# The second layer's operands moved by 32 bytes within SBUF, with the order of work left as it is

## The chip, the cores and the metric

One NeuronCore of a Trainium2 chip runs the whole program. The metric is the device time of one execution in microseconds; the kernel before takes 1753.78 us, the median of three runs (1752.92 to 1754.33).

## The reference

Attention whose keys and values are averaged over groups of eight positions, and then two dense layers on its output, all in float32:

```python
# attention: batch 8, heads 8, sequence 576, head size 64
k_p = k.reshape(B, H, S // 8, 8, D).mean(axis=3)
v_p = v.reshape(B, H, S // 8, 8, D).mean(axis=3)
attn = softmax(q @ k_p.T / sqrt(D))
x = (attn @ v_p)            # 4608 tokens x 512
# first layer
h = np.maximum(x @ w1_in, 0.0)      # 512 -> 2048
x = h * h @ w1_out                  # 2048 -> 512
# second layer
h = x @ w2_in
out = np.maximum(0.01 * h, h) @ w2_out
```

## The kernel before

Every float32 operand of a large product is split in two parts, a rounded one ("high") and the remainder ("low"), both stored as four-byte `float32r`. A product is then three passes of TensorE: high by high, low by high, high by low.

**First layer and attention** (to about 990 us). Tokens go in nine blocks of 512. `first` (line 861) makes one chunk of 128 hidden rows by twelve matmuls of 512 columns (line 866), with the weights `wi` as the loaded operand and `xh`, `xl` as the moving one. `second` (line 894) takes the squared chunk `gh`, `gl` as the moving operand and the weights `wo` as the loaded one, again twelve matmuls of 512 columns (line 905). Attention of the next block (transposes of 128 columns in lines 449, 551, 650 and 656 and scores of 144 columns in line 587, all in plain float32; values in lines 701 to 704) stands between them, piece by piece.

**Second layer** (class `Second`, line 1124; from about 994 us to the end). The hidden dimension is taken in two halves, the tokens in six spans of 768, and each half of the weights in four pairs; that makes 48 groups. A group has seven products (`product`, line 1273: a scheme that gets a 2 by 2 block product out of seven smaller ones). Each is six matmuls of 384 columns (line 1280) with `wi` loaded and the sums of token blocks `fh`, `fl` moving: 48 x 7 x 6 = 2016 matmuls. Between the products of a group stand the six pieces of the group before (`piece`, line 1341): each is six matmuls of 512 columns (line 1347) with `sh`, `sl`, the hidden values after the leaky step, loaded and the output weights `wo` moving: 48 x 6 x 6 = 1728 matmuls. ScalarE and VectorE take the products out of PSUM (lines 1293, 1297, 1304), apply the leaky step (line 1321) and split the result (lines 1325, 1328). The order is written out by hand (`manual_schedule`); no planner moves anything.

**Places in SBUF.** Pools on the left grow from the low addresses up, pools on the right from the top down. The top of the right side lies 32 bytes past a multiple of 64. Line 82 puts a tile of 32 bytes (`pad`) there first, so that all the tiles below it start at a multiple of 64. Every operand that TensorE reads, in both layers, then starts at 0 mod 64. The weights' slots `wi0` to `wi7` and `wo0` to `wo3` are used by the first layer and then again by the second (`make_in`, line 1201, and `fetch_out`, line 1232); `sh` and `sl` lie in a pool of their own (`open_work`, line 1141), in the room that `wo4` to `wo7` had.

Of the kernel before, what the change touches and what calls it, by code (L numbers as in the profile page):

```python
# [9 lines left out]
F32 = mybir.dt.float32  # L10
F32R = mybir.dt.float32r
# [5 lines left out]
P = 128  # L17
# [26 lines left out]
def attention_relu2_leaky_kernel(  # L44
# [12 lines left out]
    nc = tc.nc  # L57
# [21 lines left out]
    ).split()  # L79

    common = ctx.enter_context(tc.tile_pool(name="sb", bufs=1, side="left"))
    pad = ctx.enter_context(tc.tile_pool(name="pad", bufs=1, side="right"))
    nc.gpsimd.memset(pad.tile([P, 8], F32, tag="pad", name="pad"), 0.0)
    weights = ctx.enter_context(tc.tile_pool(name="wt", bufs=1, side="right"))
    spare = tc.alloc_tile_pool(name="sp", bufs=1, side="right")
    attn = tc.alloc_tile_pool(name="at", bufs=1, side="left")
    opened = [spare, attn]
    psum = ctx.enter_context(tc.tile_pool(name="ps", bufs=1, space=bass.MemoryType.PSUM))
    dram = ctx.enter_context(tc.tile_pool(name="dr", bufs=1, space=bass.MemoryType.DRAM))

    BUFS = {"raw": 3, "val": 3, "qt": 2, "r": 3, "gh": 2, "gl": 2, "s": 2, "kt": 2, "kp": 2}
    BUFS.update({"m": 4, "l": 4, "st": 3, "val": 2})

    POOLS = {tag: weights for i in range(FC // 2) for tag in (f"wi{i}", f"wo{i}")}
    POOLS.update({f"wo{i}": spare for i in range(FC // 4, FC // 2)})
    POOLS.update({tag: common for tag in "cst raw r gh gl st xh xl".split()})

    def sb(shape, dt, tag):
        pool = POOLS.get(tag, attn)
        return pool.tile(shape, dt, tag=tag, name=tag, bufs=BUFS.get(tag, 1))  # L100

    def bank():
        return psum.tile([P, 512], F32, tag="ps", name="ps", bufs=4)

    def acc_bank(m):
        return psum.tile([P, 512], F32, tag=f"acc{m}", name=f"acc{m}")

    def f32(ap):
        return ap.bitcast(F32)
# [7 lines left out]
    mid = dram.tile([2, FC, P, T], F32, tag="mid", name="mid")  # L117

    cst = sb([P, C_N], F32, "cst")
    ident = cst[:, C_ID : C_ID + P]  # L120

# [6 lines left out]
    def home_tile(shape):  # L128
        return sb(shape, F32, f"wo{late.pop()}")
# [12 lines left out]
    def load_to(key, fn, tag):  # L142
        live[tag] = live.get(tag, 0) + 1
        t = sb([P, 512], F32, tag)
        fn(t)
        raws[key] = t, tag
# [5 lines left out]
    def load(n=99):  # L152
        while n and todo and not held:
            key, fn, tag = todo[0]
            if live.get(tag, 0) == BUFS[tag]:
                return
# [940 lines left out]
    def run(blk):  # L1097

        last = blk == BLOCKS - 1
        steps, turn = [], []  # L1100
        if not last:
            steps, turn = all_steps[blk + 1], value_steps(blk + 1, (blk + 1) * T)

        def chunk_done(what, c):
            if last:
                layer2.early(what, c)
            else:
                w2.tick()
                if blk == BLOCKS - 2 and (what, c) == ("out", FC - 1):
                    w2.finish()  # L1110

        block(blk, blk * T, steps, turn, chunk_done)
# [11 lines left out]
    class Second:  # L1124
# [16 lines left out]
        def open_work(self):  # L1141
# [12 lines left out]
            POOLS.update({"u3": pool, "h11": pool})  # L1154
            BUFS.update({"u3": 2, "h11": 2})
            self.acc = [acc_bank(m) for m in range(KC)] + [bank() for _ in range(2)]
# [44 lines left out]
        def make_in(self, p):  # L1201
            ra, rb = self.words
            sums = sb([P, 4, 2, P], F32, "sums")
            s1, s2, s3, s4 = (sums[:, n] for n in range(4))
            hi = sb([P, 7, 2, P], F32R, f"wi{2 * p}")
            lo = sb([P, 7, 2, P], F32R, f"wi{2 * p + 1}")
            self.weights[p] = hi, lo
            parts = (
                (slice(0, 1), ra[:, :, 0:1].rearrange("p k j f -> p j k f")),
                (slice(1, 3), rb.rearrange("p k j f -> p j k f")),  # L1210
                (slice(3, 7), sums),
            )

            def add(out_, x, y, op):
                return lambda: nc.vector.tensor_tensor(out=out_, in0=x, in1=y, op=op)

            def high(at, x):
                return lambda: nc.scalar.copy(hi[:, at], x)

            sub = ALU.subtract  # L1220
            return (
                [
                    add(s1, ra[:, :, 1], rb[:, :, 1], ALU.add),
                    add(s3, ra[:, :, 0], ra[:, :, 1], sub),
                    add(s2, s1, ra[:, :, 0], sub),
                    add(s4, rb[:, :, 0], s2, sub),
                ]
                + [high(at, x) for at, x in parts]
                + [add(lo[:, at], x, f32(hi[:, at]), sub) for at, x in parts]
            )  # L1230

        def fetch_out(self, half, p):
            t = sb([P, 2, 1024], F32R, f"wo{p}")
            nc.sync.dma_start(out=f32(t), in_=w2_parts[PAIRS * half + p])
            self.outs[p] = t.rearrange("p n (c f) -> p n c f", c=2)

# [164 lines left out]
        def run(self):  # L1401
            opened.pop().release()
            self.open_work()
            for g in range(len(self.groups)):
                self.group(g)
            self.flush()
            for i in range(TT):
                self.piece(len(self.groups) - 1, i)
            while opened:
                opened.pop().release()  # L1410
# [3 lines left out]
    with tc.manual_schedule():  # L1414
        nc.sync.dma_start(out=cst, in_=consts)
        nc.gpsimd.memset(f32(v_rem), 0.0)
        start()
        for s in value_steps(0, 0):
            s()
        pooled.add(1)  # L1420
        held.append(True)
        all_steps = {i: attention_steps(i, i * T, ("raw",)) for i in range(2, BLOCKS)}
        first_products()
        second_products()
        for blk in range(2, BLOCKS):
            run(blk)
        layer2.run()
# [31 lines left out]
```

## Time and profile before

| what | value |
| --- | --- |
| median of three runs | 1753.78 us |
| the profiled execution's own time | 1752.09 us |
| span of its instructions | 1750.2 us |
| TensorE matmuls busy | 1704.1 us, 97% of the span |
| VectorE busy | 1111.6 us, 64% |
| ScalarE busy | 627.7 us, 36% |
| GpSimd busy | 19.0 us, 1% |

The profiled execution took 1752.09 us, of which 1.9 us lie outside the span. A matmul's busy time overlaps the next one's, since they are pipelined; how often TensorE starts a matmul is read from the chain of work, where each stretch of matmuls has its length and its count.

### The profile page before, as it was taken

The numbers are of one execution on the slowest core, as the hardware profiler recorded it, in microseconds if no ns is written. First come the engines' busy times: TensorE is split into PE (matmuls) and PEld (weight loads), VectorE is DVE, ScalarE is ACT, GpSimd is POOL, SyncE is SP. The second block draws the span as 40 slices with busy tenths as digits, with TensorE's granted clock in tenths as the row PEclk, the third lists the DMA queues.
The fourth block names the chain that finished last, engine by engine and source line by source line (L and its number), as shares of the span: only waits on it lengthen the run. The fifth ranks groups of instructions, "written<-read, shape, count | busy, mean of one in ns | idle before, by whom it ended". The sixth has DMA issues, their size and how long they took to land.

```text
span 1750.2 us, 21697 instructions
## 1 busy us (share of the span) xinstructions
PE 1704.1 (97%) x8312; PEld 1462.5 (84%) x8312; DVE 1111.6 (64%) x2020; ACT 627.7 (36%) x1496; POOL 19.0 (1%) x38
## 2 busy tenths in 40 slices
PE   6889999999999999999999999999999999999999
PEld 5768778888888888888888898888888888888987
DVE  7888777666657676565435555565566665666564
ACT  4545333343443433433333322332332332233221
POOL 0012000000000000000000000000000000000000
PEclk9999999999999999999999999999999999999999
DMA  8914552323223232231004202201202411320220
GB/s 235 340 70 144 168 175 93 94 79 99 83 97 104 96 95 78 88 107 61 13 24 159 82 1 73 73 12 61 73 24 97 169 52 57 109 106 9 103 73 37
DMA packets 106296, 162.44 MB, mean 93 GB/s; under 512 B 44112, under 2 KB 44240, under 8 KB 105168
## 3 DMA queue, kind: packets, MB, share of 16 engines
q1 hardware_dynamic: 103632, 152.67, 26.3%
q0 software_dynamic: 2560, 8.39, 1.3%
q8 instruction: 65, 1.06, 0.3%
q14 instruction: 39, 0.32, 0.1%
HBM read 111.75 MB, written 49.28 MB: 92 GB/s over the span
## 4 chain that ended last, share of the span: by engine, by line
PE 90%; DVE 6%; ACT 2%; DMA 1%; issue 1%; SPq 0%; DVEq 0%; ACTq 0%
PE acc L905 20%; PE ps L1280 20%; PE ps L866 17%; PE acc L1347 15%; PE ps L1347 8%; PE acc L866 4%; PE ps L587 2%; PE ps L650 1%; PE ps L551 1%; ACT s L608 1%; PE acc L381 1%; PE ps L702 0%; DMA wi<-in_moe_w_in 0%; PE ps L704 0%; PE ps L701 0%
## 5 line engine op out<-in xcount | busy, mean ns | idle before, releaser
L905 PE MATMUL acc<-gh,wo 128*128 128x512 f32 x1152 | 298.3, 397 | 4.0 <-DVE gh L884 1.9
L866 PE MATMUL ps<-xh,wi 128*128 128x512 f32 x896 | 297.0, 394 | 0.0
L1280 PE MATMUL ps<-fh,wi 128*128 128x384 f32 x1344 | 288.3, 335 | 0.1
L1280 PEld LDWEIGHTS ps<-fh,wi 128*128 128x128 f32 x1344 | 243.1, 188 | 25.4 <-DVE gh L1293 0.4
L905 PEld LDWEIGHTS acc<-gh,wo 128*128 128x128 f32 x1152 | 214.8, 190 | 51.1 <-DVE gh L884 4.0
L1347 PE MATMUL acc<-wo,sh 128*128 128x512 f32 x768 | 208.4, 393 | 0.0
L866 PEld LDWEIGHTS ps<-xh,wi 128*128 128x128 f32 x896 | 168.2, 188 | 34.9 <-issue 0.2
L866 PE MATMUL ps<-xl,wi 128*128 128x512 f32 x448 | 174.5, 389 | 0.0
L884 DVE CAST gh<-r 128x512 fp32r<-128x512 f32 x112 | 47.7, 426 | 199.3 <-ACT r L879 199.0
L1280 PE MATMUL ps<-fl,wi 128*128 128x384 f32 x672 | 170.5, 334 | 0.0
L905 PE MATMUL acc<-gl,wo 128*128 128x512 f32 x576 | 160.8, 393 | 0.0
L1347 PEld LDWEIGHTS acc<-wo,sh 128*128 128x128 f32 x768 | 141.3, 188 | 17.2
L876 ACT ACTIVATE r<-ps 128x512 f32<-128x512 f32 x112 | 67.7, 604 | 212.1 <-PE ps L866 212.1
L905 PEld LDWEIGHTS acc<-gl,wo 128*128 128x128 f32 x576 | 109.3, 190 | 23.5
L1347 PE MATMUL acc<-wo,sl 128*128 128x512 f32 x384 | 121.8, 398 | 0.0
L1280 PEld LDWEIGHTS ps<-fl,wi 128*128 128x128 f32 x672 | 121.3, 188 | 0.0
L608 ACT ACTIVATE s<-ps,m 128x72 f32<-128x72 f32 x240 | 72.3, 331 | 104.7 <-DVE m L599 104.7
L1347 PE MATMUL ps<-wo,sh 128*128 128x512 f32 x384 | 104.2, 393 | 0.0
L1293 DVE TENSOR_TENSOR u<-gh,ps 128x384 f32<-128x384 f32 x48 | 26.6, 554 | 121.8 <-PE ps L1280 121.8
L866 PEld LDWEIGHTS ps<-xl,wi 128*128 128x128 f32 x448 | 84.2, 188 | 16.6
L1347 PEld LDWEIGHTS acc<-wo,sl 128*128 128x128 f32 x384 | 71.9, 187 | 18.9 <-DVE sl L1328 3.0
L885 DVE TENSOR_TENSOR gl<-r,gh 128x512 fp32r<-128x512 f32 x112 | 77.6, 693 | 7.7 <-PE acc L905 0.5
(205 smaller groups left out, 2364.9 us busy)
## 6 DMA issues: line engine op xcount, KB each, us to landing
wi<-in_moe_w_in SPq DMA_DIRECT2D x8, 1024.0 KB
wo<-in_moe_w_out SPq DMA_DIRECT2D x8, 1024.0 KB
val<-in_moe_w_in SPq DMA_DIRECT2D x16, 512.0 KB
val<-in_moe_w_out SPq DMA_DIRECT2D x16, 512.0 KB
w2p<-val SPq DMA_DIRECT2D x16, 512.0 KB
wo<-w2p SPq DMA_DIRECT2D x8, 1024.0 KB
xh<-x SPq DMA_DIRECT2D x10, 768.0 KB
xl<-x SPq DMA_DIRECT2D x10, 768.0 KB
```

The costliest lines, as they stand in the source:

```text
L381: nc.tensor.matmul(ps[:n, c * 2 * D : (c + 1) * 2 * D], lhsT=ident[:n, :n], rhs=raw[:n, r * 2 * D : (r + 1) * 2 * D], start=r == 0, stop=r ...
L551: nc.tensor.transpose(ps[:, cc * P : (cc + 1) * P], raw[:, cc * P : (cc + 1) * P], ident)
L587: nc.tensor.matmul(ps[: r0 + n, c2 * PAIR : (c2 + 1) * PAIR], lhsT=qt[:, cc, : r0 + n], rhs=kts[b][:, keys], start=True, stop=True,)
L608: nc.scalar.activation(out=s[:, g, :], in_=ps[:, h * SP : (h + 1) * SP], func=AF.Exp, bias=m[:, g : g + 1], accum_out=None if i in early e ...
L866: nc.tensor.matmul(ps, lhsT=w[:, kc], rhs=x[kc], start=(kc == 0 and n == 0), stop=(kc == KC - 1 and n == 2),)
L876: nc.scalar.activation(out=r, in_=ps, func=AF.Relu)
L884: nc.vector.tensor_copy(gh, r)
L885: nc.vector.tensor_tensor(out=gl, in0=r, in1=f32(gh), op=ALU.subtract)
L905: nc.tensor.matmul(acc[m], lhsT=w[:, m * P : (m + 1) * P], rhs=x, start=(c == 0 and n == 0), stop=(c == FC - 1 and n == 2),)
L1280: nc.tensor.matmul(at, lhsT=w[:, FORMS[j], kc], rhs=x[j][:, kc], start=m == 0 and j in (0, 1, 4), stop=m == 5, skip_group_check=True,)
L1293: nc.vector.tensor_tensor(out=out_, in0=x, in1=at, op=ALU.add)
L1347: nc.tensor.matmul(self.acc[i], lhsT=x[g % 2][c][t][:, at], rhs=self.outs[p][:, part_, c], start=p == 0 and m == 0, stop=p == PAIRS - 1 an ...
```

## The change

The tile `pad` is left out, so that the right side starts 32 bytes past a multiple of 64. The slots of `wo0` to `wo3` and of `wi3` become 32 bytes longer, and a tile takes its place in such a slot either at its start or 32 bytes further on (`off`, in words of four bytes). A last tile of 32 bytes is added to the pool of `sh` and `sl`, which puts the other tiles of that pool 32 bytes past a multiple of 64; it is set to zero once, on GpSimd, after the first group. The tiles `m` and `l` of attention (maxima and sums, 32 bytes each) get two buffers each in place of four, 128 bytes less in all.

Start of TensorE's operands in the built programs, in bytes past a multiple of 64:

| matmuls | moving, before | moving, after | loaded, before | loaded, after |
| --- | --- | --- | --- | --- |
| line 866 (first layer) | `xh`, `xl`: 0 | 0 | `wi`: 0 | 0 |
| line 905 (first layer) | `gh`, `gl`: 0 | 0 | `wo`: 0 | 0 |
| line 1280 (second layer) | `fh`, `fl`: 0 | 0 | `wi`: 0 | 32 |
| line 1347 (second layer) | `wo`: 0 | 32 | `sh`, `sl`: 0 | 32 |

Taken by 128 bytes, all of them stand at 64 before. After, a quarter of the loads of line 905 (those of `wo2`) start at 0 mod 128; those of line 1280 at 96, the moving operand of line 1347 at 32 for half of the matmuls and at 96 for the other half.

The order of instructions on TensorE, VectorE, ScalarE and the DMA queue of SyncE is the same in both programs, row by row, with the same waits; VectorE and ScalarE each wait once for GpSimd's count of 1 where it was 2. Only on GpSimd does one instruction move. Its start in the program before (`v_rem` is zeroed for attention, `mid` is the first layer's hidden chunks on their way to DRAM):

```order
L1438 MEMSET const-uint8-127 128x1
L1455 UNCONDITIONAL_BRANCH
L83 MEMSET pad 128x8
L1416 MEMSET v_rem 128x512
L1056 DMA mid<-r 128x512 x20
```

The same engine in the changed program, from its start to its end:

```order
L1453 MEMSET const-uint8-127 128x1
L1470 UNCONDITIONAL_BRANCH
L1431 MEMSET v_rem 128x512
L1068 DMA mid<-r 128x512 x20
L1068 DMA mid<-xl 128x512 x4
L1068 DMA mid<-xh 128x512 x4
L1068 DMA mid<-xl 128x512 x4
L1420 MEMSET off 128x8
```

A memset of eight words per partition goes from the start of GpSimd's queue to its end, behind the last of its transfers.

```diff
     common = ctx.enter_context(tc.tile_pool(name="sb", bufs=1, side="left"))
-    pad = ctx.enter_context(tc.tile_pool(name="pad", bufs=1, side="right"))
-    nc.gpsimd.memset(pad.tile([P, 8], F32, tag="pad", name="pad"), 0.0)
     weights = ctx.enter_context(tc.tile_pool(name="wt", bufs=1, side="right"))
...
-    BUFS = {"raw": 3, "val": 3, "qt": 2, "r": 3, "gh": 2, "gl": 2, "s": 2, "kt": 2, "kp": 2}
-    BUFS.update({"m": 4, "l": 4, "st": 3, "val": 2})
+    BUFS = {"raw": 3, "val": 3, "qt": 2, "r": 3, "gh": 2, "gl": 2, "s": 2, "kt": 2, "kp": 2, "m": 2, "l": 2}
+    BUFS.update({"st": 3, "val": 2})
...
-    def sb(shape, dt, tag):
+    OFF = 8
+
+    def sb(shape, dt, tag, off=None):
         pool = POOLS.get(tag, attn)
-        return pool.tile(shape, dt, tag=tag, name=tag, bufs=BUFS.get(tag, 1))
+        if off is None:
+            off = OFF if tag in ("wo1", "wo3") else 0
+        n = int(np.prod(shape[1:]))
+        size = [P, OFF + n] if off or tag == "wi3" else shape
+        t = pool.tile(size, dt, tag=tag, name=tag, bufs=BUFS.get(tag, 1))
+        if size is shape:
+            return t
+        t = t[:, off : off + n]
...
-            hi = sb([P, 7, 2, P], F32R, f"wi{2 * p}")
-            lo = sb([P, 7, 2, P], F32R, f"wi{2 * p + 1}")
+            hi = sb([P, 7, 2, P], F32R, f"wi{2 * p}", OFF)
+            lo = sb([P, 7, 2, P], F32R, f"wi{2 * p + 1}", OFF)
...
-            t = sb([P, 2, 1024], F32R, f"wo{p}")
+            t = sb([P, 2, 1024], F32R, f"wo{p}", OFF * (1 - p % 2))
...
                 self.group(g)
+                if g == 0:
+                    last = opened[-1].tile([P, OFF], F32, tag="off", name="off")
+                    nc.gpsimd.memset(last, 0.0)
```

## Rows read from the trace of the kernel before

**Rows 1.** The page's busy times, share of span and instructions; granted clock in 40 slices.

```profile
PE 1704.1 (97%) x8312; PEld 1462.5 (84%) x8312; DVE 1111.6 (64%) x2020; ACT 627.7 (36%) x1496; POOL 19.0 (1%) x38
...
PEclk9999999999999999999999999999999999999999
```

**Rows 2.** Busy time by stretch, first and second layer: us; engines (instructions); clock, DMA.

```profile
300.00:990.00 690.00, 680.63 (x3235) 565.28 (x3234) 415.06 (x819) 271.36 (x756) 0.00 (x0) 1.00 0.26 83
994.00:1740.00 746.00, 745.91 (x3718) 668.70 (x3717) 450.94 (x795) 218.19 (x408) 0.00 (x0) 1.00 0.19 68
```

**Rows 3.** Who waited for whom from 994 us on: us, times, longest us.

```profile
DVE u L1293 <- PE ps L1280: 170.9, 95, 3.8
ACT sh L1325 <- DVE h L1321: 126.8, 48, 3.0
...
PEld acc L1347 <- DVE sl L1328: 3.0, 11, 0.4
...
PEld ps L1280 <- DVE gh L1293: 0.4, 1, 0.4
```

**Rows 4.** The chain in the second layer: start us, length us, matmuls.

```profile
1401.44 1.39 PE acc L1347 x6
1402.83 1.04 PE ps L1280 x6
1403.87 1.39 PE ps L1347 x6
...
1407.69 2.08 PE ps L1280 x12
1409.78 1.39 PE acc L1347 x6
```

**Rows 5.** The chain at the end of the first layer, with scores and transposes between.

```profile
863.84 0.98 PE ps L587 x8
864.82 2.78 PE ps L866 x12
867.60 2.72 PE acc L905 x12
870.32 2.72 PE ps L866 x12
873.04 2.72 PE acc L905 x12
875.76 0.44 PE ps L551 x4
```

**Rows 6.** The page's groups of the second layer's matmuls and weight loads, with counts.

```profile
L1280 PE MATMUL ps<-fh,wi 128*128 128x384 f32 x1344 | 288.3, 335 | 0.1
L1280 PEld LDWEIGHTS ps<-fh,wi 128*128 128x128 f32 x1344 | 243.1, 188 | 25.4 <-DVE gh L1293 0.4
L1347 PE MATMUL acc<-wo,sh 128*128 128x512 f32 x768 | 208.4, 393 | 0.0
...
L1280 PE MATMUL ps<-fl,wi 128*128 128x384 f32 x672 | 170.5, 334 | 0.0
...
L1347 PE MATMUL acc<-wo,sl 128*128 128x512 f32 x384 | 121.8, 398 | 0.0
...
L1347 PE MATMUL ps<-wo,sh 128*128 128x512 f32 x384 | 104.2, 393 | 0.0
```

**Rows 7.** Single lines, ns min/median/max, first and last start: `pad`, the fetch of `wo`, `sl`.

```profile
L83 POOL MEMSET pad<- x1: 105/105/105, 0.7 to 0.7; 128x8 f32 x1
...
L1234 SPq DMA_DIRECT2D wo<-w2p x8: 319/320/383, 920.5 to 1377.7; - x8
...
L1328 DVE TENSOR_TENSOR sl<-h,sh x48: 549/551/552, 1000.2 to 1733.9; 128x384 fp32r<-128x384 f32 x48
```

More of the change, by code (lines that the diff above doesn't have):

```diff
@@ L96, in attention_relu2_leaky_kernel @@
     POOLS.update({tag: common for tag in "cst raw r gh gl st xh xl".split()})
-    def sb(shape, dt, tag):
+    OFF = 8
+    def sb(shape, dt, tag, off=None):
         pool = POOLS.get(tag, attn)
-        return pool.tile(shape, dt, tag=tag, name=tag, bufs=BUFS.get(tag, 1))
+        if off is None:
[6 more added lines that the diff above has]
+        t = t[:, off : off + n]
+        if len(shape) == 2:
+            return t
+        names = "abcd"[: len(shape) - 1]
+        sizes = {a: k for a, k in zip(names, shape[1:])}
+        return t.rearrange(f"p ({' '.join(names)}) -> p {' '.join(names)}", **sizes)
     def bank():
```

## The prediction

> **What bounds the kernel now.** I read the busy times first, then the two layers apart, then who waits for whom, and last the chain of work, whose stretches give the time from one matmul's start to the next.
>
> TensorE is busy for 97% of the span at its full granted clock [rows 1]. The reader should see where the rest is: in the first layer 680.6 of 690 us, in the second 745.9 of 746 [rows 2]. From 994 us on TensorE never stands still. VectorE and ScalarE are the ones that wait there, for TensorE or for each other, in waits of up to 3.8 us; the two waits that hold up TensorE's weight loads come to 3.4 us in sum, the longest 0.4 us, and none of it shows as idle time of the matmuls [rows 2, 3]. So in the second layer the time is the number of matmuls times their pitch, and no other engine's speed counts until it gets worse by more than those waits.
>
> The pitch comes from the chain. A piece of six matmuls of 512 columns takes 1.39 us, 231.7 ns each; six of 384 columns take 1.04 us, 173.3 each [rows 4]. In the first layer a dozen of 512 columns takes 2.72 us, 226.7 each, once it runs undisturbed; the dozen right behind the scores takes 2.78, 231.7 each, although it reads the same kind of tiles at the same places [rows 5]. From 384 to 512 columns the settled pitch goes from 173.3 to 226.7: 53.4 ns for 128 columns, 0.417 ns a column, one column per clock at 2.4 GHz, the level that the rows grant [rows 2, 4, 5]. At that rate 512 columns are 213.3 ns and 384 are 160. Both leave the same **excess of 13.3 ns**, whatever the columns; and unsettled stretches of 512 leave 18.3.
>
> What the excess hangs on is half visible. Every matmul loads its weights, a load per matmul [rows 1]; the load of 128 columns lasts 188 ns and lies beside the stream of the matmul before [rows 6]. Matmuls in plain float32 have loads too, but stream at half the rate: eight of 144 columns take 0.98 us and four of 128 take 0.44, so 122.5 and 110 ns, against 120 and 106.7 at two clocks a column [rows 5]. Their excess is about 2.5 to 3.3 ns. I read this so: the excess is not the change of weights as such, but what a load costs a stream that already reads at its full rate. That it is 18.3 or 13.3 at equal places shows that the two readers' step against each other counts as well.
>
> **The change, part by part.**
>
> The order: it stays. TensorE, VectorE, ScalarE and SyncE issue the same rows with the same waits, so no wait is added, no queue is passed, and nothing is newly hidden or uncovered by order. The two buffers for `m` and `l` add no wait either. Cost: nothing.
>
> The memset: 105 ns leave the start of GpSimd [rows 7] and stand at its end, behind its last transfer, with nobody waiting for it. `v_rem` is zeroed 0.1 us sooner, and its readers come much later. Cost: nothing.
>
> VectorE, ScalarE and the fetches of `wo` now write and read at 32 mod 64 in the second layer. No operand of theirs with this shape stands there before, so the price is bounded: `sl` takes 551 ns [rows 7] and is the one that TensorE's loads wait for, 11 times, 0.4 us at most [rows 3]. If each such step took a tenth more, 55 ns at the late ones, TensorE would wait 11 x 55 ns = 0.6 us more. As a gain it is worth nothing, since TensorE does not idle. I take 0. The last fetch is issued at 1377.7 us [rows 7] for a pair whose products come a group later; that covers it.
>
> The first layer: its operands stay at 0 mod 64. The loads of `wo2` go from 64 to 0 mod 128, 432 matmuls. The trace shows one place only among these; I take 0, with 1 ns either way, 0.4 us.
>
> The second layer's 3744 matmuls are the change. 2016 of line 1280 get the loaded operand at 32 while the moving one stays at 0; 1728 of line 1347 get both at 32. Nothing that TensorE reads before lies off a multiple of 64, so the trace does not show the price and I bound it from both sides.
>
> Below nothing: if the half-line between load and stream keeps them out of each other's way, line 1280's excess falls to that of the half-rate rows, 13.3 to 2.5 ns: 2016 x 10.8 = 21.8 us less [rows 4 to 6]. A smaller gain is that line 1347 runs at the settled pitch: 1728 x (231.7 - 226.7) = 8.6 us less.
>
> Above nothing: suppose SBUF is read in lines of 64 bytes, the unit of the change (no row shows one). A load of 512 bytes that starts in the middle of a line then touches nine lines and not eight. If the excess goes by lines, it grows by an eighth, 1.7 ns: 3744 x 1.7 = 6.2 us more. The moving 2048 bytes of line 1347 touch 33 lines and not 32; if a line costs its full time, 213.3 / 32 = 6.7 ns, that adds 1728 x 6.7 = 11.5 us, 17.7 in all.
>
> The value I take: the only change of this excess that the trace shows between two states of like matmuls is 5.0 ns [rows 5]. I let one of the two lines lose that much, 8.6 us (line 1347) or 10.1 us (2016 x 5.0, line 1280), so 9.3. Why down: all pairs now start in step, which is the most crowded place for two readers; a half-line apart is the only relation that changes, and some 11 of the 13.3 ns are what half-rate streams do not pay.
>
> The sum: the span falls from 1750.2 to 1740.9, the profiled execution's 1752.1 to 1742.8. Its median stands 1.7 us above that execution, so 1753.8 - 9.3 = **1744.5 us**.
>
> **A rule that speaks against it.** The row shows 13.3 ns of excess for 384 and for 512 columns alike [rows 4, 5]. The Trainium skill, TensorE: Matmul & The Clock Gate, section Step-by-step: what each phase is for, says that TensorE reads its moving operand and its weights through two independent ports, and that loading the next weights takes nothing from the running matmul. By that rule the place of the one against the other cannot matter, and the time stays at 1753.8, as in the rival of no change. The trace agrees only for half-rate streams. SBUF — State Buffer of the Trainium skill, section Door 1: The DMA port swizzle, gives SBUF lines of 16 bytes; by it a start at 32 crosses no more lines than one at 0, which speaks against the slower rival below. No row here shows a line's length.
>
> **The rivals.**
>
> Slower: the crossing of lines. Place: the loads of both lines and the moving operand of line 1347. Price: 6.2 us for the loads alone, time 1760; with the stream 17.7, time 1771.5. It decides as soon as a reader fetches whole 64-byte lines and has no slack left. For it: at one column per clock the stream has none to spare, as the excess shows, and more than half of the moved operands gain no half-line apart: in line 1347 both move together. Against it: the first layer's 13.3 ns are the same for 32 and for 24 lines of stream, so single lines of the stream are not what is paid now.
>
> No change: the excess comes of the step between load and stream in time, not of places. For it: the same places cost 226.7 or 231.7 by what ran before [rows 5], and the second layer is always unsettled since 384 and 512 columns alternate [rows 4]. Time 1753.8, give or take 2. That the change doesn't do what it says is no rival: the built program has the places of the table.
>
> Larger gain: line 1280's excess goes down to the half-rate rows' 2.5, 1753.8 - 21.8 = 1732; with line 1347 settled as well 1723. It is the far end of the forecast's own mechanism.
>
> **How the numbers follow.** Faster 0.5: 0.36 about the forecast (1738 to 1750), 0.08 about the larger gain, 0.06 between. No change 0.2. Slower 0.3: 0.2 about 1760, 0.1 towards 1771. A tenth at either end is left out, so the range goes from 1735, short of the larger gain, to 1763, past the price of the loads. The forecast's own range is 1738 to 1750. A measurement of this kernel can tell 0.2%, 3.5 us, from no change; the forecast and both slower prices lie beyond that, so the chances are 0.5, 0.2 and 0.3.
>
> **What would show it.** In the changed kernel's chain: a piece of line 1280 at 1.01 us and not 1.04 (168.3 ns), or one of line 1347 at 1.36 and not 1.39, means the forecast; 1.05 and 1.40 to 1.44 means the crossing of lines; the same lengths mean the step in time. In the first layer the dozens must stay at 2.72, and TensorE must stay busy for the whole stretch from 994 us; if it idles there, a slower write at 32 is the cause and this argument is wrong. It is wrong too if line 1280 gets slower and line 1347 faster, since I give no reason for that.

## The result, and the profile after

The changed kernel takes 1766.61 us (median of four runs, 1765.68 to 1766.76) against 1753.85 for the kernel before (the median of four runs as well): 1.0072 times as long, with a 95% interval of 1.0055 to 1.009. It is 12.8 us slower. The prediction said 1744.5, with 1735 to 1763 as its range.

The page of the changed kernel, the lines that answer to [rows 1] (busy us, share of the span and instructions; granted clock in 40 slices), and its span:

```profile
span 1763.8 us, 21701 instructions
...
PE 1722.5 (98%) x8312; PEld 1471.5 (83%) x8312; DVE 1111.9 (63%) x2020; ACT 627.3 (36%) x1496; POOL 18.9 (1%) x38
...
PEclk9999999999999999999999999999999999999999
```

The other engines are as busy as before, and the clock is the same. TensorE has as many matmuls and 18 us more of busy time. Nor does it stand still in the second layer, or wait more for others: the stretch of [rows 2] and the waits of [rows 3] from 994 us on read, in the changed kernel, whose second layer starts at about 1005 us (us and instructions by engine; us, times and longest us of a wait):

```profile
994.00:1740.00 746.00, 745.95 (x3701) 668.81 (x3700) 450.52 (x794) 220.18 (x410) 0.00 (x0) 1.00 0.19 68
```

```profile
PEld acc L1359 <- DVE sl L1340: 2.8, 11, 0.4
...
PEld ps L1292 <- DVE gh L1305: 0.4, 1, 0.4
```

So it is the pitch, and the place is a surprise. In the last block of the first layer nothing of attention stands between the matmuls; there the kernel before runs every dozen in the same time. Its chain (start us, length us, matmuls):

```profile
925.87 2.72 PE ps L866 x12
928.59 2.72 PE acc L905 x12
931.31 2.72 PE ps L866 x12
```

The chain of the changed kernel in the same block. Line 878 has chunks 5 and 6 here and line 917 chunks 4 and 5; further down they have 9 and 10, and 8 and 9:

```profile
941.48 2.79 PE ps L878 x12
944.27 2.79 PE acc L917 x12
947.07 2.79 PE ps L878 x12
949.86 2.75 PE acc L917 x12
...
963.64 2.73 PE ps L878 x12
966.37 2.80 PE acc L917 x12
969.16 2.76 PE ps L878 x12
971.92 2.80 PE acc L917 x12
```

The first layer is slower, though all its operands stay at 0 mod 64. The reader is to see the change of sides. In the first half of the block all the `wi` dozens (line 878 of the changed kernel, 866 before) take 2.79 to 2.80 us; in the second half the `wo` dozens (917, 905 before) do. Chunks 0 to 7 load `wi0` to `wi3` and `wo0` to `wo3`, chunks 8 to 15 the other eight. The tiles with the longer pitch are `wi0` to `wi3` and `wo4` to `wo7`: by all starts of the trace they went from 227.9 to 232.5 ns a matmul, 8.8 us in sum. These eight tiles lie 128 bytes lower than before. The other eight went from 227.7 to 229.0 ns, 2.2 us, though six of them lie where they lay; most of their dozens take 2.75 to 2.76 us between the slow ones. One dozen stands out among them: the 2.79 us at 944.27 is chunk 4 of `wo2`, which lies 64 bytes lower.

That follows from the room. In the built program before, every split operand of both layers starts at 192 modulo 256 bytes, the moving ones on the left like the loaded ones on the right. Five slots longer by 32 bytes, less the pad of 32, displace what lies below all of them by 128 bytes; `wo2` and `wo3`, which lie between, by 64; the other six stay. So the quarter of line 905's loads that starts at 0 mod 128, 432 matmuls, is that of `wo2` and `wo3` together, and not of `wo2` alone.

The second layer's chain in the changed kernel, to be held against [rows 4]:

```profile
1400.11 1.06 PE ps L1292 x6
1401.17 1.40 PE ps L1359 x6
1402.57 1.06 PE ps L1292 x6
...
1409.55 1.39 PE acc L1359 x6
1410.95 1.04 PE ps L1292 x6
1411.99 1.38 PE acc L1359 x6
```

Pieces of 384 columns take 1.04 to 1.06 us and those of 512 columns 1.38 to 1.40: on balance a little more than the 1.04 and 1.39 of before.

All starts of the trace give the split. The table has the time from each matmul's start to the next one's, summed by line, in us; its last three columns are mean pitches in ns, without the long gaps in which TensorE waited (over 260 ns, or 210 for 384 columns). Lines are named as in the kernel before, and the experiments' rows stand here too:

| kernel | first layer (866, 905) | line 1280 | line 1347 | 866 | 1280 | 1347 |
| --- | --- | --- | --- | --- | --- | --- |
| before | 821.8 | 351.1 | 401.0 | 227.6 | 174.0 | 231.5 |
| changed | 832.9 | 353.5 | 401.1 | 230.6 | 175.2 | 231.7 |
| e1, m and l | 822.8 | 351.1 | 401.0 | 227.6 | 174.0 | 231.5 |
| e2, wi +32 | 821.9 | 354.3 | 399.9 | 227.7 | 175.6 | 231.0 |
| e3, right side 128 lower | 835.7 | 353.8 | 397.1 | 232.3 | 175.3 | 229.2 |
| e4, wi 64 to 256 | 822.1 | 353.5 | 400.7 | 227.7 | 175.2 | 231.4 |
| e5, room without 32 | 832.0 | 354.8 | 401.2 | 230.6 | 175.8 | 231.7 |
| e6, right side 32 higher | 838.6 | 351.3 | 394.3 | 233.0 | 174.1 | 227.1 |
| e7, right side 64 lower | 824.9 | 349.7 | 398.0 | 229.6 | 173.3 | 229.5 |
| e8, half of sh, sl 128 lower | 821.5 | 353.7 | 401.1 | 227.7 | 175.3 | 231.5 |
| e9, x 32 off | 822.6 | 351.3 | 394.2 | 227.6 | 174.1 | 227.0 |
| e10, x 32 off, other way | 822.8 | 356.4 | 395.9 | 227.6 | 176.6 | 228.5 |
| e11, x 64 off | 822.8 | 356.1 | 393.6 | 227.6 | 176.5 | 227.1 |
| e12, x 32 off, sh and sl 128 | 822.6 | 351.6 | 399.1 | 227.6 | 174.2 | 230.4 |

Of the changed kernel's loss 11.0 us lie in the first layer and 2.5 us in the second.

### The profile page after: what moved, and what is told of

Its sections match the earlier page's. It is cut to its first block, busy times and chain, and to the rows that moved or that the text cites. A ratio compares the mean times of both kernels' runs of the same rounds, so it can differ in the third digit from the quotient of the medians.

```text
span 1763.8 us, 21701 instructions
## 1 busy us (share of the span) xinstructions
PE 1722.5 (98%) x8312; PEld 1471.5 (83%) x8312; DVE 1111.9 (63%) x2020; ACT 627.3 (36%) x1496; POOL 18.9 (1%) x38
## 3 DMA queue, kind: packets, MB, share of 16 engines
q8 instruction: 65, 1.06, 0.3%
## 4 chain that ended last, share of the span: by engine, by line
PE 92%; DVE 5%; ACT 2%; issue 0%; DMA 0%; SPq 0%; DVEq 0%; ACTq 0%
PE acc L917 21%; PE ps L1292 20%; PE ps L878 18%; PE acc L1359 15%; PE ps L1359 8%; PE acc L878 4%; PE ps L599 2%; PE ps L662 1%; PE ps L563 1%; PE acc L393 1%; PE ps L714 0%; DVE xl L691 0%; PE ps L716 0%; PE ps L715 0%; PE ps L713 0%
## 5 line engine op out<-in xcount | busy, mean ns | idle before, releaser
L917 PE MATMUL acc<-gh,wo 128*128 128x512 f32 x1152 | 302.8, 401 | 3.8 <-DVE gh L896 1.7
```

Source lines behind the costliest of these rows:

```text
L917: nc.tensor.matmul(acc[m], lhsT=w[:, m * P : (m + 1) * P], rhs=x, start=(c == 0 and n == 0), stop=(c == FC - 1 and n == 2),)
```

## Experiments

Some words first: a stream is the moving operand as TensorE reads it, the load beside it is that of the next matmul's weights, and their distance is the start of the load less the start of the stream, modulo 256 bytes. A piece's last stream has a load of the other line beside it, and so has a product's; that place is called the hand-over. The theory (A): a matmul's pitch depends on the distance of load and stream, modulo some 256 bytes, and the displaced tiles of the first layer make the loss. Rivals: the fewer buffers of attention (B), the 32 bytes themselves (C), and the prediction's own rivals.

**The two buffers alone.** The tiles behind `m` and `l` move down, nothing else.

```diff
-    BUFS.update({"m": 4, "l": 4, "st": 3, "val": 2})
+    BUFS.update({"m": 2, "l": 2, "st": 3, "val": 2})
```

> The kernel before with two buffers for m and l in place of four, and nothing else: the attention tiles behind them lie 128 bytes lower, every other tile stays. Theory A (the loss of the changed kernel comes of loads that were displaced by 64 or 128 bytes against the stream they lie beside): 1754, within 2 us. Theory B (the loss of 11 us in the first layer comes of the attention's fewer buffers or moved tiles): about 1765.

1753.62 us against 1753.85, ratio 0.9999 (0.999 to 1.0008). B falls.

**The second layer's weights alone.** `wi` has 1024 bytes to spare in its slots in the second layer, so it can move without longer slots.

```diff
-            hi = sb([P, 7, 2, P], F32R, f"wi{2 * p}")
+            hi = form_tile(f"wi{2 * p}", (8, 8, 8, 8)[p])
...
+    def form_tile(tag, off):
+        t = sb([P, off + 14 * P], F32R, tag)[:, off:]
+        return t.rearrange("p (a b c) -> p a b c", a=7, b=2)
```

(`lo` likewise.)

> The kernel before with the second layer's wi put 32 bytes further on inside its slot, which has the room; pad, m, l, wo, sh and sl as before. Theory A: 32 bytes alone cost little, line 1280 goes from 173.6 to at most 174.3 ns: 1754 to 1756. The prediction's forecast: 10 us less, 1744. The prediction's rival of crossed lines: 2016 x 1.7 ns, 1757.

1756.26 us, ratio 1.001 (1.0001 to 1.0018). Line 1280 goes to 175.6 ns, more than A allowed, line 1347 falls by half a nanosecond. The forecast's gain of 10 us does not come from this; the size alone would also fit the crossing of lines, against which e5 and e6 speak.

**Everything on the right 128 bytes lower.**

```diff
-    nc.gpsimd.memset(pad.tile([P, 8], F32, tag="pad", name="pad"), 0.0)
+    nc.gpsimd.memset(pad.tile([P, 40], F32, tag="pad", name="pad"), 0.0)
```

(with two buffers for `m` and `l`, which give the room)

> The kernel before with two buffers for m and l and a pad of 160 bytes in place of 32: every tile on the right lies 128 bytes lower, all of them still at 0 mod 64. Theory A: all loads of the first layer whose stream lies on the left run at about 232.7 ns and not 226.9, as wi0 to wi3 and wo4 to wo7 do in the changed kernel: some 3300 x 5.5 = 18 us more, and line 1280 some 2.5 ns more, 5 us; line 1347, where load and stream move together, stays; in the block whose stream lies in wo7 the pitch stays too. 1774 to 1779. If only places mod 64 count: 1754.

1766.99 us, ratio 1.0072 (1.0059 to 1.0086). No operand has left 0 mod 64, and it costs as much as the change did. The first layer's chain now has one pitch for all chunks:

```profile
926.38 2.79 PE acc L905 x12
929.17 2.79 PE ps L866 x12
931.96 2.78 PE acc L905 x12
```

2.79 us are 232.5 ns a matmul, where the kernel before has 226.7. The run has its own control: in the block whose moving operand lies in `wo7`, on the right like the loads and displaced with them, the matmuls that stream from it keep 228.0 ns (227.0 before), while the rest of line 866 stands at 232.6. That control is good for this distance only: in e6 and e7, where the same tiles move together by 32 and 64 bytes, these matmuls have 230.7 and 231.8 ns. One in three matmuls of that block streams from the left, at a changed distance, and stands among them.

The sum was set too high (1774 to 1779). The first layer rose by 13.8 us and not 18, line 1280 by 2.8 and not 5, and line 1347 got faster by 3.9 us, with its own operands displaced together.

VectorE and ScalarE read and write SBUF too, and their tiles lie otherwise against TensorE's here. The trace shows no part of theirs: from 925 to 1000 us line 866 takes 232.5 ns a matmul where VectorE is busy for over 95% of it (63 matmuls) and 232.5 where it is for under 5% (77).

**Four displacements in one kernel.**

```diff
-            hi = form_tile(f"wi{2 * p}", (8, 8, 8, 8)[p])
+            hi = form_tile(f"wi{2 * p}", (16, 32, 48, 64)[p])
```

> The kernel before with the second layer's wi put 64, 128, 192 and 256 bytes further on for pairs 0, 1, 2 and 3. Theory A with a period of 256 bytes: pair 3 at the 173.3 ns of before, pair 1 the slowest with 2 to 4 ns more, pairs 0 and 2 between; 1756 to 1759. With a period of 128 bytes pairs 1 and 3 are as before; if displacement counts without a period, pair 3 is the slowest.

1755.23 us, ratio 1.0012 (1.0003 to 1.0021). For the low weights, which load in the middle of a product, pairs 0 to 3 have 175.1, 177.9, 173.3 and 173.9 ns against 173.3 to 173.5 before. 128 bytes are the slowest and 256 nearly as before, so the period is not 128. But 192 bytes (pair 2) are as before in these two places too. Over all six matmuls of a product the pairs have 174.9, 175.9, 175.3 and 174.5 ns against 174.0, and only there is 256 the nearest. That the period is 256 rests on this one pair, and is not shown.

**The room without the 32 bytes.** The changed kernel, with the second layer's tiles left at 0 mod 64:

```diff
-            hi = sb([P, 7, 2, P], F32R, f"wi{2 * p}", OFF)
+            hi = sb([P, 7, 2, P], F32R, f"wi{2 * p}", 0)
...
-        size = [P, OFF + n] if off or tag == "wi3" else shape
+        size = [P, OFF + n] if off or tag in ("wi3", "wo0", "wo2") else shape
...
-            t = sb([P, 2, 1024], F32R, f"wo{p}", OFF * (1 - p % 2))
+            t = sb([P, 2, 1024], F32R, f"wo{p}")
...
-                if g == 0:
-                    last = opened[-1].tile([P, OFF], F32, tag="off", name="off")
-                    nc.gpsimd.memset(last, 0.0)
```

(`lo` likewise.)

> The changed kernel with its longer slots and its missing pad, but nothing put 32 bytes further on in the second layer: wi, wo, sh and sl stand at 0 mod 64 there as well, and the displacements of 64 and 128 bytes between the tiles stay. Theory A (displacement makes the loss): 1764 to 1768, the first layer as in the changed kernel. Theory C (the 32 bytes make it, the displacement only shifts it about): 1754 to 1757.

1766.87 us, as much as the changed kernel's 1766.61; ratio to before 1.008 (1.0066 to 1.0093). The pattern of the last block is the changed kernel's own:

```profile
940.80 2.79 PE ps L878 x12
943.59 2.79 PE acc L917 x12
...
962.96 2.73 PE ps L878 x12
965.68 2.79 PE acc L917 x12
```

This settles the loss: the longer slots, with the pad gone, make it, and the 32 bytes that they are for change nothing on top that these runs can tell. C falls. The crossing of lines falls as a cause too: no operand leaves 0 mod 64 here.

**No pad.** Everything on the right 32 bytes higher, in both layers.

```diff
-    pad = ctx.enter_context(tc.tile_pool(name="pad", bufs=1, side="right"))
-    nc.gpsimd.memset(pad.tile([P, 8], F32, tag="pad", name="pad"), 0.0)
```

> The kernel before without its pad: every tile on the right lies 32 bytes higher, in both layers, so the loads of lines 866, 905 and 1280 lie 32 bytes off their streams, and line 1347 moves as a whole; no other displacement. It is the second layer's half-line without the room. Theory A: line 1280 as in the run with wi 32 bytes further on, 175.6 ns (3 us more), line 1347 the same or up to 1 ns less; in the first layer 228 to 230 ns and not 227.8: 1757 to 1762. The prediction's rival of crossed lines: 1.7 ns on 7200 loads, 1766. Its forecast: faster than 1754.

1763.3 us, ratio 1.0056 (1.0043 to 1.0069). The two layers go opposite ways. Its chain in the first layer and in the second:

```profile
926.39 2.80 PE acc L903 x12
929.19 2.80 PE ps L864 x12
...
1402.67 1.05 PE ps L1278 x6
1403.72 1.36 PE ps L1345 x6
1405.08 2.08 PE ps L1278 x12
1407.17 1.36 PE acc L1345 x6
```

The first layer loses 16.7 us, at 233.3 ns a matmul. The second gains 6.5 us, all of it in line 1347 of the kernel before (1345 here): 1.36 us a piece and not 1.39, 227.1 ns. Here both operands of that line start in the middle of 64 bytes. So this is what the second layer can gain from 32 bytes, if `wi`, the leaky values and the moved `wo` keep their places against each other. A's numbers missed: the first layer was to take 228 to 230 ns and takes 233.0, line 1280 was to take 175.6 and stays at 174.1, and the time lies just past the 1757 to 1762.

**Everything on the right 64 bytes lower.**

```diff
-    nc.gpsimd.memset(pad.tile([P, 8], F32, tag="pad", name="pad"), 0.0)
+    nc.gpsimd.memset(pad.tile([P, 24], F32, tag="pad", name="pad"), 0.0)
```

(with two buffers for `m` and `l`)

> The kernel before with two buffers for m and l and a pad of 96 bytes in place of 32: every tile on the right lies 64 bytes lower, all at 0 mod 64. Theory A: the first layer's loads off by 64 bytes at 229.3 ns, as wo2 and wo3 in the changed kernel, against 232.6 at 128: 1758 to 1762, between the kernel before and the pad of 160 bytes. If 64 bytes are a unit of their own: 1754.

1752.16 us, ratio 0.9993 (0.9984 to 1.0002): no difference. The first layer's settled dozens take 2.75 us, 229.2 ns, as expected:

```profile
927.49 2.75 PE ps L866 x12
930.24 2.75 PE acc L905 x12
```

But the sum of the first layer rises by 3 us only: starts that follow one another within 260 ns sum to 7.9 us more, and the longer gaps, in which TensorE waits, to 4.8 us less. The second layer falls by 4.4 us. The expected 1758 to 1762 was wrong: what a displacement costs in a settled row is not what it costs where lengths alternate.

**Half of the leaky values 128 bytes lower** (modulo 256). Unlike the runs above, line 1347's load is displaced against its own stream.

```diff
-                [
-                    [
-                        [pool.tile([P, TS], F32R, tag=f"{n}{k}{c}{t}", name=n) for t in range(2)]
+                        more = FILL.get((n, k)) if (c, t) == (1, 1) else 0
+                        at = pool.tile([P, TS + more], F32R, tag=f"{n}{k}{c}{t}", name=n)
+                        out_[c][t] = at[:, :TS]
...
+            FILL = {("sh", 0): 32, ("sh", 1): 32, ("sl", 0): 32, ("sl", 1): 32}
```

> The kernel before with sh and sl of every second group put 128 bytes lower, so that in line 1347 the load lies 128 bytes off the stream for pairs 1 and 3 and beside it for pairs 0 and 2; the 384-column products as before. Theory A: those 864 matmuls some 2 to 5 ns slower, 1756 to 1758. Theory D (in the second layer a displacement may also help, since line 1347 went from 231.5 to 229.2 ns when line 1280's loads were displaced by 128): 1750 to 1753.

1756.73 us, ratio 1.0018 (1.0009 to 1.0027). The total is as A said and the place is not: line 1347 keeps 231.5 ns, displaced or not, and line 1280, whose operands did not move, goes from 174.0 to 175.3. The slower products are those of pairs 0 and 2, with 176.3 and 176.7 ns; pairs 1 and 3 keep 174.0. The displaced pieces, those of pairs 3 and 1, stand just between the products of pairs 0 and 2. A disturbance is handed on to the matmuls that follow: the largest rise is in the middle of a product, 181.5 and 183.4 ns for its fourth matmul against 173.3 to 173.6 before.

**The x tiles instead of the weights.** What the right side did without its pad can be had by moving the only operand of the second layer that lies on the left, in a pool that has the room. No slot gets longer and the first layer keeps its places.

```diff
+            def form(n, j):
+                off = 56 if (n, j) == ("fh", 0) else 0
+                t = pool.tile([P, off + 2 * TS], F32R, tag=f"{n}{j}", name=n)
+                return t[:, off:].rearrange("p (k f) -> p k f", k=2)
...
-                [pool.tile([P, 2, TS], F32R, tag=f"{n}{j}", name=n) for j in range(7)]
-                for n in ("fh", "fl")
+                [form(n, j) for j in range(7)] for n in ("fh", "fl")
```

> The kernel before with the second layer's x tiles (fh, fl and the tiles behind them) 224 bytes further up, so that line 1280's loads lie 32 bytes past their streams modulo 256 and all else stays where it was: the relation that the second layer had without the pad, with no longer slots. Theory A with relations (load against stream, modulo 256, the first layer untouched): line 1280 at 174.1 ns and line 1347 at 227.1 as without the pad, 6 to 7 us less, 1747. If the place mod 64 of weights and squares themselves counts: 1754.

1747.95 us, ratio 0.9966 (0.9953 to 0.9978): faster than both kernels. Its chain in the first layer and in the second:

```profile
927.89 2.72 PE ps L866 x12
930.61 2.72 PE acc L905 x12
```

```profile
1401.23 1.04 PE ps L1285 x6
1402.27 1.36 PE ps L1352 x6
1403.63 1.05 PE ps L1285 x6
1404.68 1.36 PE ps L1352 x6
```

The first layer has its 2.72 us and the second the 1.36 of the run without the pad. The weights and the leaky values are at 0 mod 64 here and x is at 32; without the pad it was the other way about, and the pitches are the same to 0.1 ns. So the place modulo 64 of either does not count in these two lines, their distance does, and it is the same in both runs at the hand-over too.

**Other distances of x.** `off = 8` and `off = 48` in the same edit.

> The same with the x tiles 32 bytes further up, so that line 1280's loads lie 32 bytes before their streams. If the sign does not count: 1747. If it does, between 1750 and 1757; with the pad of 96 bytes, 64 bytes before the stream, the two lines took 747.7 us in sum against 752.1 before.

1754.62 us, ratio 1.0005 (0.9996 to 1.0014). The sign counts: line 1347 gains 5.1 us and line 1280 loses 5.3.

> The same with the x tiles 192 bytes further up, so that line 1280's loads lie 64 bytes past their streams. By the pad of 96 bytes (64 bytes the other way) 4 us less, 1749 to 1751, if the sign does not count.

1752.18 us, ratio 0.9988 (0.9979 to 0.9997), just past the expected end and by other shares than the pad of 96 bytes: line 1347 gains 7.4 us, line 1280 loses 5.0.

**The gain, and line 1347's distance broken.** The run with x 32 bytes off, with `sh` and `sl` 128 bytes lower.

```diff
+            FILL = {("sh", 0): 0, ("sh", 1): 0, ("sl", 0): 0, ("sl", 1): 32}
```

> The kernel of the run with x 32 bytes off, and sh and sl besides 128 bytes lower, so that line 1347's loads lie 128 bytes off their streams as half of them do in the changed kernel. Theory A: the second layer loses its 6 us again, since line 1347's own relation is broken: 1752 to 1758. If it is line 1280's relation alone that counts: 1748.

1753.13 us, ratio 0.9992 (0.9983 to 1.0001). The gain is all but gone, and line 1347 is the one that lost it, with 230.4 ns against 227.0:

```profile
1400.55 1.38 PE acc L1353 x6
1401.93 1.05 PE ps L1286 x6
1402.97 1.38 PE acc L1353 x6
```

In the changed kernel line 1347's loads lie 64, 128 or 192 bytes past their streams modulo 256, because its four `wo` slots and `sh`, `sl` were displaced by different amounts, and half of line 1280's loads lie 160 past theirs and not 32. Those 160 past have 176.0 and 176.1 ns there, those 32 past 174.4. That is the likely reason why the second layer did not get there what it gets in e9. It is not shown by itself: e12 moved the leaky values against the x streams at the hand-over as well, from 32 to 160 past, so it does not tell which of the two distances line 1347 lost its gain by.

## Why the prediction was wrong

**What bounds the kernel** held: pitch alone, no idle time, no longer waits in the second layer. The parts put at nothing held too, but for one: order, memset, buffers (e1: 1753.62 against 1753.85), and the writes at 32 mod 64 by VectorE and ScalarE (`sl` still takes 551 to 552 ns, and the wait for it stands at 2.8 us and was 3.0).

**The step that failed** is the first layer: "its operands stay at 0 mod 64 ... I take 0, with 1 ns either way, 0.4 us". It measured 11.0 us more. The prediction asked where an operand starts modulo 64, and modulo 128 for `wo2`, and took what starts there as before to be in the same place. It did not follow what five longer slots do to the tiles below them. Eight of the sixteen weight tiles moved by 128 bytes, at a price of 4.6 ns a matmul on half of the first layer's 3456; e3 shows that price for all of them at once, and e5 shows it with the 32 bytes taken out. The prediction's own sign for it came: the dozens of the first layer were to stay at 2.72 us and take up to 2.80.

**The second layer's term**, 9.3 us less, measured 2.5 us more. Its size was not far off for the clean case: e9 has 6.6 us less in these two lines (752.1 to 745.5) and 6.2 in the median. The sign that the prediction named for it, a piece of line 1347 at 1.36 us, stands in e6 and e9. The reason was right in part: the place of load and stream against each other is what the excess hangs on. It was wrong on the direction. The prediction took equal places for the most crowded ones; in the settled rows of the first layer they are the best that was measured, 226.7 ns against 229.2 to 233.3 at three other distances (e7, e3, e6). So the clean case owes its right sign in part to luck.

It was wrong, too, on which matmuls would gain. The distance changed in line 1280, and line 1280 gained nothing (174.0 to 174.1 ns); line 1347, whose own operands moved together in e6 and not at all in e9, went from 231.5 to 227.1 and 227.0, nearly the settled pitch. So its gain comes from what stands before it. In e2 line 1280 has the same distance as in e9 and stands at 175.6 ns, with line 1347 at 231.0; in e6 its operands lie at the very addresses of e2, and it stands at 174.1. What differs is the other line's places, and so the distances at the hand-over, where a load of one line lies beside a stream of the other. That these make the gain is argued from these runs; none changes them alone.

**The rivals.** The time of the slower rival, 1760 to 1771, holds the result, its mechanism does not: in e5 nothing starts off a multiple of 64 and the time is the same, and in e6 both operands of line 1347 would cross one 64-byte line more and run at 227.1 ns, faster than before. No change was to follow if the excess came of time and not of places; e3 excludes that, where places alone take 226.7 to 232.5 ns. The Trainium skill, TensorE: Matmul & The Clock Gate, section Step-by-step: what each phase is for, has the two reads on independent ports and the load taking nothing from the running matmul. The measurement differs for these full-rate streams (226.7 to 232.5 ns in e3 by places alone), and it decides. What the two reads share, the runs don't show.

**The range** ended at 1763 because its upper end was built from the second layer alone.

What stays open is the mechanism: whether and where the two reads collide, why the distances 32 past and 32 before differ, and whether the period is 256 bytes; a pair at 256 alone speaks for it. Nor does a run move the streams of the first layer with its loads in place: that distance counts there, and not the weights' own place modulo 256, is carried over from line 1347, which settles at 226.7 ns within its pieces in e3 with both operands 128 bytes lower.

## What to carry to other kernels

Before an operand is moved, list the places of all operands of the matmuls, before and after, modulo a few hundred bytes: a longer slot moves everything that lies below it, and what moves unintended can cost more than the move brings. Where TensorE runs without a pause, the distance between the loaded and the moving operand is a knob: here up to 3% of a matmul's pitch, and from 0.3% less to 0.7% more of the whole time. Turn it by moving the one operand that has room and shares no slot with other stages. A gain that a layout shows in one stage is to be taken to it with the distances of all its operands kept, those at the hand-over between lines included.

## What the runs showed of the hardware

A settled row of `float32r` matmuls of 512 columns starts one every 226.7 ns when the loaded and the moving operand start at the same place modulo 256 bytes (the kernel before). With the load 32 bytes past the stream it is 233.3 ns (e6), 64 bytes before it 229.2 (e7), 128 bytes off 232.5 (e3). Where matmuls of 384 and 512 columns alternate, the same place is not the best one: 174.0 and 231.5 ns there, against 174.1 and 227.0 with the loads of the 384-column products 32 bytes past their streams (e9). And a matmul's pitch depends on places of matmuls before it: line 1280 slowed down by 1.3 ns with none of its own operands moved, and only in the groups between whose products displaced loads stand (e8).
